# The order of VectorE's small column copies in items of one tile of a mixture-of-experts loop

## The chip, the cores and the metric

The kernel runs on one core of one Trainium2 chip. A time is the device time of one execution in microseconds (us), and a kernel's time is the median of several executions. The engines are TensorE (PE, with its weight loads PEld), VectorE (DVE), ScalarE (ACT), GpSimd (POOL) and SyncE (SP). Each takes its own instructions in order and waits on semaphores for the others.

## The reference

Attention over keys and values that are averaged in groups of 8 rows, and after it a mixture of experts in which each of the 4608 rows goes to one of 8 experts, the one with the largest gate. An expert takes at most `capacity` rows (4608 / 8 * 2 = 1152), in the order of the rows; a row beyond that stays zero.

```python
logits = x @ w_gate                       # x: 4608 x 512, from the attention
expert_idx = np.argmax(logits, axis=1)
gate_w = probs[np.arange(N), expert_idx]  # softmax of logits
...
h = np.maximum(np.einsum('ecd,edf->ecf', disp, w1), 0.0)   # 8 experts, 512 -> 1024
y = np.einsum('ecf,efd->ecd', h, w2)                       # 1024 -> 512
...
out[i] = gate_w[i] * y[expert_idx[i], pos[i]]              # zero where a row was not kept
```

## The kernel before

The first 212 us are the attention, the routing and a prologue that already computes two tiles of one expert. Behind it stands a loop (lines 1327 to 1372) over items. An item is one or two tiles of 128 rows of one expert; how many, which columns of the tables belong to it, and whether the expert changes behind it are read from the table `cf` as the loop runs, so the code of the loop has branches: `two` chooses between an item of two tiles (`hidden_all`) and of one (`hidden_one`), and `sw` says that the next item is another expert's, so that its weights are split in this one.

All matrix products are made in three terms: each operand is split into a rounded high part (names with h: `xh`, `w1h`, `hh`, `w2h`; a cast on ScalarE, line 127) and the remainder (`xl`, `w1l`, `hl`, `w2l`; a subtraction on VectorE, line 128 or 1299). TensorE multiplies high by high, high by low and low by high.

What one item does, by engine:

- TensorE: the hidden layer (line 152, or 1309 and the transposes of 1314 where there is one tile) into `ph`, for two tiles the product of tile 1 into `y1`, the transposes of the next item's rows (line 1286, `xg` into `px`), and the product of tile 0 into `y0` (line 165). The next item's hidden layer follows at once; it needs `xh` and `xl` of its rows, and after `sw` the new `w1h` and `w1l`. `w1l` is split in four instructions: two for the first 512 columns of the hidden layer and two for the rest.
- VectorE: the remainders `hl` of the hidden layer, then three small copies of int32 columns by dynamic offset: `ix`, the row numbers that the gather after next needs (128x4, line 92), `io`, the row numbers and gates of this item's own rows (128x4, line 92), and `iz`, the rows beyond capacity that get zeros (128x2, line 1360). Further the remainders `xl` of the next item's rows, after `sw` the `w1l` and `w2l`, and the gates (line 1321) that scale `y` into `ys`.
- POOL: at the item's start it overwrites `io` and `iz` with zeros (lines 1336 and 1337), which it may do once the scatters of the item before, which read `io` and `iz`, have landed. Then it makes a guard, a tiny subtraction that waits for VectorE's `ix` (line 95), issues two gathers of 128 rows into `xg` (line 97, after TensorE's transposes have read `xg`), a guard on `iz` and two scatters of zero rows, guards on `io` and on `ys`, and two scatters of result rows into `out` (line 102).
- SP: the weights of the expert after next into `r`, two loads for the first layer (line 120) and two for the second (line 124), each once VectorE's and ScalarE's splits have read `r`.

VectorE's `io` and `iz` are written after POOL's zeros, so they wait for POOL's lines 1336 and 1337. Within the loop the order of each engine's instructions is that of the code.

## Time and profile before

| | us |
|---|---|
| median of 3 runs | 639.56 |
| the three runs | 635.9, 639.56, 639.87 |
| the profiled execution | 638.75 |
| its span, from the first to the last instruction | 637.1 |
| TensorE busy in the span | 600.0 |
| VectorE busy in the span | 335.4 |
| POOL busy in the span | 315.6 |

The profile is that of one execution. The view of the waits gives for each pair of instructions what one waited for, the us in total, how many times, and the longest. A row of the timeline has the start in us from the span's start, the duration (of several instructions in a row together), the engine, the line, the operation with what it writes and reads, and how many; in brackets stands the idle time of the engine ahead of it and what ended it. A row of the busy time by stretch has the stretch, its length, and for PE, PEld, DVE, ACT and POOL the busy us and the number of instructions, then the clock granted to TensorE (1.00 is full), the share of the DMA engines and GB/s. A row of one line has the shortest, the median and the longest duration in ns, and the first and the last start.

### The profile page before, as it was taken

The page shows a single profiled execution, that of the slowest core. Times are in us where ns is not written, and L with a number is a line of the kernel's source. Part 1 is how long each engine was busy: PE and PEld are TensorE (multiplying, and loading weights), DVE is VectorE, ACT ScalarE, POOL GpSimd, SP SyncE. Part 2 cuts the span into 40 slices and gives each one's busy share as a digit, 9 for nine tenths or more (in the row PEclk, how much of TensorE's full clock was granted, in tenths as well). Part 3 has the DMA queues.
Part 4 walks back from the last instruction along what each step waited for, and adds up shares of the span by engine and source line. Part 5 has one row for each costly group of instructions (what it writes and reads, how often), then busy time and mean ns, then how long its engine had stood idle before and what let it go on. Part 6 is the DMA issues. An engine that isn't in the chain of part 4 may idle for free. (4 is left out here: it accounts for less than half of the span.)

```text
span 637.1 us, 13935 instructions
## 1 busy us (share of the span) xinstructions
PE 600.0 (94%) x3966; PEld 534.0 (84%) x3967; DVE 335.4 (53%) x742; ACT 223.1 (35%) x412; POOL 315.6 (50%) x533
## 2 busy tenths in 40 slices
PE   2799999999889899999999999999999999999994
PEld 1688889898787789988889989988899889988983
DVE  4776968888878421359447622227322584223212
ACT  2456364556532211157155412117111581101111
POOL 7399959557664331445444541444324255341344
PEclk9899999999999999999999999999999999999998
DMA  9999899485622810137728720214501261110112
GB/s 314 305 338 278 240 305 198 93 248 127 181 52 76 311 54 33 66 133 277 241 96 287 260 100 33 66 51 163 189 33 66 77 247 36 66 66 6 60 51 65
DMA packets 103744, 93.79 MB, mean 147 GB/s; under 512 B 82852, under 2 KB 82852, under 8 KB 103720
## 3 DMA queue, kind: packets, MB, share of 16 engines
q1 hardware_dynamic: 54552, 62.47, 30.4%
q0 software_dynamic: 11392, 21.57, 10.7%
q10 hardware_dynamic: 37776, 9.46, 6.8%
q8 instruction: 12, 0.20, 0.1%
q14 instruction: 12, 0.10, 0.0%
HBM read 132.96 MB, written 31.27 MB: 258 GB/s over the span
## 5 line engine op out<-in xcount | busy, mean ns | idle before, releaser
L1299 DVE SCALAR_TENSOR_TENSOR hl<-ph,hh 128x512 fp32r<-128x512 f32 x60 | 40.9, 691 | 108.0 <-ACT hh L1298 75.7
L1298 ACT ACTIVATE hh<-ph 128x512 fp32r<-128x512 f32 x60 | 36.0, 599 | 173.8 <-PE ph L152 168.2
L152 PE MATMUL ph<-xh,w1h 128*128 128x256 f32 x480 | 76.5, 281 | 2.8 <-DVEq L1327 2.5
L165 PE MATMUL y<-w2h,hh 128*128 128x512 f32 x280 | 78.1, 400 | 0.0
L165 PE MATMUL y<-w2l,hh 128*128 128x512 f32 x280 | 76.6, 395 | 0.0
L152 PE MATMUL ph<-xl,w1h 128*128 128x256 f32 x480 | 76.2, 281 | 0.4 <-DVE w1l L128 0.4
L152 PE MATMUL ph<-xh,w1l 128*128 128x256 f32 x480 | 76.1, 280 | 0.0
L97 POOL DMA_INDIRECT xg<-xs,ix x42 | 44.3, 1056 | 58.8 <-PE y L165 51.6
L165 PE MATMUL y<-w2h,hl 128*128 128x512 f32 x280 | 71.0, 396 | 0.0
L152 PEld LDWEIGHTS ph<-xh,w1h 128*128 128x128 f32 x480 | 65.8, 188 | 5.8 <-issue 4.8
L152 PEld LDWEIGHTS ph<-xl,w1h 128*128 128x128 f32 x480 | 65.1, 188 | 0.7 <-issue 0.7
L152 PEld LDWEIGHTS ph<-xh,w1l 128*128 128x128 f32 x480 | 65.1, 188 | 0.0
L165 PEld LDWEIGHTS y<-w2h,hl 128*128 128x128 f32 x280 | 52.6, 188 | 12.7
L165 PEld LDWEIGHTS y<-w2l,hh 128*128 128x128 f32 x280 | 52.6, 188 | 12.6
L549 PE MATMUL pa<-vbd,pT 126*128 126x146 f32 (+5 forms) x400 | 58.2, 306 | 1.1 <-DVE pairs L704 0.7
L165 PEld LDWEIGHTS y<-w2h,hh 128*128 128x128 f32 x280 | 50.0, 188 | 9.4
L549 PEld LDWEIGHTS pa<-vbd,pT 126*128 126x128 f32 (+1 forms) x400 | 54.7, 179 | 3.5 <-issue 1.7
L128 DVE TENSOR_TENSOR xl<-px,xh 128x512 fp32r<-128x512 f32 x40 | 25.7, 685 | 56.8 <-ACT xh L127 56.8
L95 POOL TENSOR_TENSOR guard<-ix 128x4 int32<-128x4 int32 x21 | 6.1, 292 | 99.9 <-DVE ix L92 87.6
L538 ACT COPY pT<-pp 126x384 f32<-126x384 f32 x72 | 30.5, 424 | 68.6 <-PE pp L537 53.4
L513 PE MATMUL ps<-kbs,qT 128*128 128x144 f32 (+1 forms) x320 | 52.0, 305 | 1.9 <-ACT qT L504 1.9
L102 POOL DMA_INDIRECT out_dram<-zrow,iz x40 | 45.9, 1147 | 15.8 <-issue 15.2
(263 smaller groups left out, 1021.6 us busy)
## 6 DMA issues: line engine op xcount, KB each, us to landing
r<-in_moe_w_dram SPq DMA_DIRECT2D x84, 1024.0 KB
raw<-in_k_dram SPq DMA_DIRECT2D x12, 768.0 KB
raw<-in_v_dram SPq DMA_DIRECT2D x12, 768.0 KB
qblk<-in_q_dram SPq DMA_DIRECT2D x32, 256.0 KB
xs<-xo ACTq DMA_DIRECT2D x16, 512.0 KB
raw<-in_moe_w_dram SPq DMA_DIRECT2D x4, 512.0 KB
r<-in_moe_w_dram SPq DMA_DIRECT2D x4, 512.0 KB
qtail<-in_q_dram SPq DMA_DIRECT2D x8, 128.0 KB
```

Of the source, the lines that this page charges most:

```text
L95: nc.gpsimd.tensor_sub(guard, ix, ix)
L97: nc.gpsimd.indirect_dma_start(out=dst[:, i, :].bitcast(F32), out_offset=None, in_=src, in_offset=bass.IndirectOffsetOnAxis(ap=ix[:, i, 0: ...
L102: ins = nc.gpsimd.indirect_dma_start(out=out[:, :], out_offset=bass.IndirectOffsetOnAxis(ap=i_, axis=0), in_=src, in_offset=None, bounds_c ...
L128: eng.tensor_sub(lo, src, hi.bitcast(F32))
L152: nc.tensor.matmul(p[:, f2], a[:, c, f * P : (f + 1) * P], b[:, c], start=(f2 == 0 and j == 0 and c == 0), stop=(f2 == 1 and j == 2 and c ...
L165: nc.tensor.matmul(y, a[:, c, i * P : (i + 1) * P], b[:, c], start=(first and n == 0), stop=(last and n == len(terms) - 1))
L513: nc.tensor.matmul(self.ps[us, h, 0 : 2 * SP_].rearrange("p (a x) -> p a x", a=2), self.qT[:, h, us], kbs[b // 2 % 2][:, :, b % 2, h], sta ...
L538: nc.scalar.copy(self.pT[:, cs.start : cs.stop], pp[0:KC, 0 : len(cs)])
L549: made = nc.tensor.matmul(self.pa[us, h0 * XW : (h0 + nh) * XW], self.pT[:, c, us], vbd[b % 2][:, c, 0:nh].rearrange("r s x -> r (s x)"), ...
L1298: nc.scalar.activation(hh[s], p, AF.Relu)
L1299: nc.vector.scalar_tensor_tensor(out=hl[s], in0=p, scalar=0.0, in1=hh[s].bitcast(F32), op0=ALU.max, op1=ALU.subtract)
```

## The change

In items of one tile VectorE's copy of `ix` moves from behind the remainders `hl` to the very start of the item. Its copies of `io` and `iz` move from behind the split of the first weights to right after `hl`, ahead of the remainders `xl` of the next rows. In items of two tiles only `iz` moves: from behind the gate of tile 1 to ahead of it. No instruction is added or taken away, apart from branches; no transfer changes.

```diff
-                def next_x():
+                def next_ids():
                     columns(ix, ids[:, ds(c2, 2), :])
-                    gather(xg, ix, xs[:, :])
-                    split_x()
+
+                def own_ids():
+                    columns(io, ids[:, ds(ct, 2), :])
+                    nc.vector.tensor_scalar(out=iz, in0=idd[:, ds(cd, 2)], scalar1=0, scalar2=None, op0=ALU.bitwise_or)
...
                     with tc.If(sw > 0):
                         split_w1()
-                    next_x()
-                    columns(io, ids[:, ds(ct, 2), :])
+                    next_ids()
+                    gather(xg, ix, xs[:, :])
+                    split_x()
+                    own_ids()
                     gate(1)
                 with both.Else():
+                    next_ids()
                     hidden_one()
-                    next_x()
+                    gather(xg, ix, xs[:, :])
+                    own_ids()
+                    split_x()
                     with tc.If(sw > 0):
                         split_w1()
-                    columns(io, ids[:, ds(ct, 2), :])
                 load_w1(we, cond=nw > 0, bounds_check="skip_entire_dma")
-                nc.vector.tensor_scalar(out=iz, in0=idd[:, ds(cd, 2)], scalar1=0, scalar2=None, op0=ALU.bitwise_or)
```

VectorE in the branch for one tile, from the remainders `hl` on, as it was. In the brackets are the engines and the DMA queues that a row waits for; REGISTER_ALU and ISA rows only prepare a wait or an offset:

```order
L128 TENSOR_TENSOR hl<-ph_2826,hh 128x4x128 [waits Activation_I-2847_own]
L128 REGISTER_ALU
L128 TENSOR_TENSOR hl<-ph_2827,hh 128x4x128 [waits Activation_I-2847_own]
L92 ISA
L92 TENSOR_SCALAR ix<-ids 128x4 [waits DMASW0_I-2847_own,DMASW1_I-2847_own,DVE_I-2847_own,Pool_I-2847_own]
L128 REGISTER_ALU
L128 TENSOR_TENSOR xl<-px_2822,xh 128x4x128 [waits Activation_I-2847_own]
L128 REGISTER_ALU
L128 TENSOR_TENSOR xl<-px_2823,xh 128x4x128 [waits Activation_I-2847_own]
L1356 COMPARE_AND_BRANCH
```

The same branch of VectorE now, from its start on:

```order
L92 TENSOR_SCALAR ix<-ids 128x4 [waits DMASW0_I-2847_own,DVE_I-2847_own,DMASW1_I-2847_own,Pool_I-2847_own]
L128 REGISTER_ALU
L128 TENSOR_TENSOR hl<-ph_2826,hh 128x4x128 [waits Activation_I-2847_own]
L128 REGISTER_ALU
L128 TENSOR_TENSOR hl<-ph_2827,hh 128x4x128 [waits Activation_I-2847_own]
L92 ISA
L92 TENSOR_SCALAR io<-ids 128x4 [waits DMASW4_I-2847_own,DMASW5_I-2847_own,DVE_I-2847_own,Pool_I-2847_own]
L1344 ISA
L1344 TENSOR_SCALAR iz<-idd 128x2 [waits DMASW3_I-2847_own,DMASW2_I-2847_own,Pool_I-2847_own]
L128 REGISTER_ALU
L128 TENSOR_TENSOR xl<-px_2822,xh 128x4x128 [waits Activation_I-2847_own]
```

`ix` stands ahead of `hl`, and `io` and `iz`, with their waits for the landing of scatters (DMASW4 and 5, DMASW3 and 2) and for POOL, stand ahead of `xl` and so ahead of the `w1l` that follow `xl`.

TensorE at the start of the hidden layer of an item of two tiles, as it was:

```order
L152 MATMUL ph_2824<-xh,w1l 128x256 [waits DVE_I-2847_own]
L152 MATMUL ph_2824<-xh,w1l 128x256
L152 REGISTER_ALU
L152 MATMUL ph_2824<-xh,w1l 128x256 [waits DVE_I-2847_own]
L152 MATMUL ph_2824<-xh,w1l 128x256
L152 REGISTER_ALU
L152 MATMUL ph_2824<-xl,w1h 128x256 [waits DVE_I-2847_own,DVE_49]
L152 MATMUL ph_2824<-xl,w1h 128x256 x3
```

And the same place now:

```order
L152 MATMUL ph_2824<-xh,w1l 128x256 [waits DVE_I-2847_own]
L152 MATMUL ph_2824<-xh,w1l 128x256
L152 REGISTER_ALU
L152 MATMUL ph_2824<-xh,w1l 128x256 [waits DVE_I-2847_own]
L152 MATMUL ph_2824<-xh,w1l 128x256
L152 MATMUL ph_2824<-xl,w1h 128x256 [waits DVE_49]
L152 MATMUL ph_2824<-xl,w1h 128x256 x3
L152 MATMUL ph_2824<-xh,w1h 128x256 x4
```

TensorE's matmuls stand as before; the first of the `xl` group no longer waits for a count of VectorE within the loop, since the waits of the `w1l` group ahead of it, one for each half of the rows of the first weights, cover it.

## The prediction

> **What bounds the kernel now.** I read four views: the page's first lines, the waits of each engine from 212 us on (the loop over the items), the busy time by stretch, and then the timeline around each item of one tile. Times with three digits before the point are us from the start of the span.

> ```profile
> span 637.1 us, 13935 instructions
> PE 600.0 (94%) x3966; PEld 534.0 (84%) x3967; DVE 335.4 (53%) x742; ACT 223.1 (35%) x412; POOL 315.6 (50%) x533
> ...
> PE ph L152 <- DVEq L1327: 2.5, 1, 2.5
> PE ph L152 <- DVE w1l L128: 0.4, 2, 0.2
> ...
> POOL guard L95 <- DVE ix L92: 87.6, 16, 12.2
> POOL io L1336 <- DMA out_dram<-ys,io: 59.2, 19, 6.3
> ...
> 299.00:326.00 27.00, 27.00 (x161) 23.65 (x161) 10.86 (x16) 5.22 (x10) 15.56 (x25) 1.00 0.66 226
> ...
> L128 DVE TENSOR_TENSOR hl<-ph,hh x10: 681/692/692, 291.5 to 622.9; 128x512 fp32r<-128x512 f32 x10
> ```

> In the loop TensorE is the bound: its only waits on another engine are 2.5 us as the loop begins and two waits on `w1l`, 0.4 us together; the stretch from 299 to 326 us is full of matmuls. So what delays TensorE moves the end by as much, and what frees another engine is worth nothing until the last item, where TensorE runs out of work. POOL idles 87.6 us for VectorE's index columns and 59.2 us for the landing of the scatters, off that path. The ten `hl` splits of line 128 are two for each item of one tile: five such items. In order of time I call them A (292 us), B (328), C (434), D (517) and E (623). In A to D the next expert's first weights are split too; E is the last item and splits none.

> **Part 1: `io` and `iz` stand ahead of the remainders `xl`.** VectorE takes its instructions in order. The new `io` must wait until POOL has zeroed `io` (L1336), and that waits for the landing of the item before's result rows. Behind it now stand two `xl` and four `w1l`. Item A before, by engine and start:

> ```profile
> 286.82 1.80 POOL L102 DMA_INDIRECT out_dram<-ys,io  x1 [0.15 <-issue]
> 291.45 1.29 DVE L128 TENSOR_TENSOR hl<-ph,hh 128x512 fp32r<-128x512 f32 x2 [1.43 <-ACT hh L127]
> 292.73 1.28 DVE L128 TENSOR_TENSOR xl<-px,xh 128x512 fp32r<-128x512 f32 x2
> 293.93 4.62 DVE L128 TENSOR_TENSOR w1l<-r,w1h 128x1024 fp32r<-128x1024 f32 x4
> 294.24 0.96 POOL L1336 TENSOR_TENSOR io<-zi 128x4 int32<-128x4 int32 x1 [5.62 <-DMA out_dram<-ys,io]
> 295.15 1.18 POOL L1337 TENSOR_TENSOR iz<-zi 128x2 int32<-128x2 int32 x1
> 296.73 0.63 PE L152 MATMUL ph<-xh,w1l 128*128 128x256 f32 x4
> 297.56 0.72 PE L152 MATMUL ph<-xl,w1h 128*128 128x256 f32 x4 [0.20 <-DVE w1l L128]
> ```

> VectorE reaches this place at 291.45 + 1.29 = 292.74. POOL's zeroing starts at 294.24 only, 5.62 us after the scatter's issue ended (286.82 + 1.80 = 288.62). Nothing ahead of that landing is changed, so I keep 294.24. POOL's two zeroings took 0.96 and 1.18 here, beside a `w1l`; with VectorE waiting I take the 0.19 that they need in item E (below), the second 0.15 after the first: done at 294.58. A hand-over from VectorE to POOL costs 0.14 there; I take the same the other way, and 0.07 from the last column to the next instruction: the first `xl` starts at about 294.24 + 0.55 = 294.79. From `xl`, the first `w1l` follows after 1.20 (293.93 - 292.73), the next after 1.135 (4.62 less one of 1.22, by 3), so the second `w1l`, which completes the first half of the weights, ends 3.55 after `xl`. TensorE reads that half in the third and fourth matmul of its `w1l` group, and the `xl` group starts 0.24 later. With 0.14 for the hand-over, the `xl` group starts at the landing + 0.55 + 3.55 + 0.14 + 0.24 = landing + 4.48 = 298.72, where before it started at 297.56. Its old wait of 0.20 is inside that, since the order of TensorE shows that group's own wait gone. **A: +1.16.** That the index columns come first takes away 0.07 of VectorE's time there, inside the same sum.

> Item D is the same case:

> ```profile
> 512.30 1.80 POOL L102 DMA_INDIRECT out_dram<-ys,io  x1 [0.15 <-issue]
> 516.93 1.29 DVE L128 TENSOR_TENSOR hl<-ph,hh 128x512 fp32r<-128x512 f32 x2 [1.42 <-ACT hh L127]
> 518.20 1.28 DVE L128 TENSOR_TENSOR xl<-px,xh 128x512 fp32r<-128x512 f32 x2
> 520.09 0.58 POOL L1336 TENSOR_TENSOR io<-zi 128x4 int32<-128x4 int32 x1 [5.99 <-DMA out_dram<-ys,io]
> 522.24 0.63 PE L152 MATMUL ph<-xh,w1l 128*128 128x256 f32 x4
> 523.03 0.71 PE L152 MATMUL ph<-xl,w1h 128*128 128x256 f32 x4 [0.16 <-DVE w1l L128]
> ```

> VectorE is there at 516.93 + 1.29 = 518.22, the rows land for 520.09, TensorE's group starts at 520.09 + 4.48 = 524.57 and not at 523.03. **D: +1.54.**

> In B and C POOL has zeroed long before VectorE comes:

> ```profile
> 325.45 0.19 POOL L1336 TENSOR_TENSOR io<-zi 128x4 int32<-128x4 int32 x1 [1.88 <-DMA out_dram<-ys,io]
> 328.69 0.16 DVE L92 TENSOR_SCALAR ix<-ids 128x4 int32 x1
> 328.76 1.28 DVE L128 TENSOR_TENSOR xl<-px,xh 128x512 fp32r<-128x512 f32 x2
> 329.91 0.98 POOL L97 DMA_INDIRECT xg<-xs,ix  x1 [0.71 <-PE y L165]
> 330.06 4.66 DVE L128 TENSOR_TENSOR w1l<-r,w1h 128x1024 fp32r<-128x1024 f32 x4
> 333.62 0.64 PE L152 MATMUL ph<-xh,w1l 128*128 128x256 f32 x4
> ```

> In B the zeroings end by 325.45 + 0.34 = 325.79 and VectorE comes at 328.69, a cover of 2.9 us; C goes like B. Two column instructions cost 0.07 to 0.25 ahead of `xl`; the second `w1l` ended at 330.06 + 1.22 + 1.14 = 332.42 and TensorE came to it at 333.62 + 0.24, so 1.4 us of cover is left: **0**. If that cover were gone, the cost would be at most those 0.25.

> What stands behind `w1l` on VectorE comes later by as much as `xl`, 294.79 - 292.73 = 2.06 us: the gate of the result, the `w2l` splits, and with the splits SP's two weight loads, which wait until they free their buffers. In A:

> ```profile
> 299.44 4.62 DVE L128 TENSOR_TENSOR w2l<-r,w2h 128x1024 fp32r<-128x1024 f32 x4
> 309.13 1.09 PE L165 MATMUL y<-w2l,hh 128*128 128x512 f32 x4
> ```

> The last `w2l` would end at 299.44 + 4.62 + 2.06 = 306.12, and TensorE reads the first at 309.13, itself 1.16 later: a cover of 4 us. The loads are wanted at the next split of first weights, at 330.06: **0**. In items of two tiles `iz` goes ahead of the gate of tile 1, one instruction of 0.16 ahead of a result that only POOL's scatter reads: **0**.

> **Part 2: the next index columns come first.** POOL can issue the two gathers as soon as it has zeroed and TensorE has transposed the rows. For TensorE this is early by tens of us in A to D: 0. It counts in E, where POOL's chain ends the program:

> ```profile
> 619.53 1.00 POOL L102 DMA_INDIRECT out_dram<-ys,io  x1 [2.04 <-issue]
> 622.40 0.19 POOL L1336 TENSOR_TENSOR io<-zi 128x4 int32<-128x4 int32 x1 [1.88 <-DMA out_dram<-ys,io]
> 622.55 0.19 POOL L1337 TENSOR_TENSOR iz<-zi 128x2 int32<-128x2 int32 x1
> 623.54 0.16 DVE L92 TENSOR_SCALAR ix<-ids 128x4 int32 x1
> 623.84 0.20 POOL L95 TENSOR_TENSOR guard<-ix 128x4 int32<-128x4 int32 x1 [1.10 <-DVE ix L92]
> 624.76 0.98 POOL L97 DMA_INDIRECT xg<-xs,ix  x1 [0.72 <-PE y L165]
> 627.94 0.75 DVE L1321 TENSOR_SCALAR ys<-y,io 128x512 f32<-128x512 f32 x1 [2.18 <-PE y L165]
> 631.30 0.21 POOL L1371 TENSOR_TENSOR guardf<-ys 128x2 f32<-128x2 f32 x1
> 631.67 1.00 POOL L102 DMA_INDIRECT out_dram<-ys,io  x1 [0.16 <-issue]
> ```

> POOL is free at 622.55 + 0.19 = 622.74 and waits 1.10 for the columns made at 623.54 (end 623.70, then 0.14 to POOL's start: the hand-over above). With columns made ahead of the item's own remainders, the guard starts at 622.75, and all behind it moves by 1.09: POOL is busy or in short issue gaps from there to 631.67. The last scatter needs VectorE's gate, done at 627.94 + 0.75 = 628.69; it would start at 630.58, so the cover is 1.9 us. **E: -1.09.** What could lessen it is the first gather's own wait, 0.72, which the row puts down to TensorE. Bounds 0 and -1.09; I take the full one, since B's gather stands 0.71 behind its guard too, which looks like a fixed gap and not like a wait that ends by chance.

> **The sum** is 1.16 + 1.54 - 1.09 = +1.61 us on the profiled execution of 638.75 (span 637.1 and 1.65 around it): 640.4. That execution lies 0.81 below the median of the three runs, 639.56; they spread from 635.9 to 639.87. About 1% (6.4 us) is what a measurement of this kernel can tell from no change.

> [...] The landing of 5.6 and 6.0 us is the weightiest row: E has 1.88. [...] The second row is B's gather at 329.91, started 0.15 ahead of a `w1l`. [...]

> **The rivals.**
> 1. The scatters land early in A and D, as in E. Then neither item waits, 0.20 and 0.16 of old waits go, and E gains: 638.75 - 0.36 - 1.09 = 637.3. It decides when the landing in A is before 293.1. Against it: the scatters and the weight loads beside them are issued by the item before, where nothing of this changes. 0.12.
> 2. POOL's gap of 2.04 us ahead of its scatter at 619.53, put down to nothing but issue (0.16 ahead of the last one), is not met again, and E starts 1.88 earlier on POOL. The last scatter can then come no earlier than the gate lets it: 628.69 + 0.14 + 0.37 from its guard's start = 629.20, a gain of 2.47 in place of 1.09: 639.0. 0.10.
> 3. The first gather of E is held by TensorE, not by VectorE: E gains nothing: 641.45. 0.08.
> 4. Gathers and `w1l` take turns in A and D. The gathers now come at about 295.5 (294.58 + 0.20 + 0.71) and a gather later, on top of the first two `w1l`: up to 0.98 more in each item, 640.4 + 1.96 = 642.4. Against it: B's `w1l` that started 0.15 into a gather. 0.05.
> 5. Slower by over 1%, by one mechanism: VectorE's wait for the landing is much longer than before's trace has it. Over 1% needs +1.16 + 1.54 to become 7.5, 2.4 us more in each: landings 8.0 and 8.4 us after the issue. The longest wait of POOL for a landing is 6.3 (the row above); with that in both items the time is only 0.68 + 0.31 more, 641.4. 0.04.

> **How the numbers follow.** The forecast, a stall in A and D less the gain in E, has 0.60; the five rivals 0.39; 0.01 is left for what I have not seen. The range runs from rival 1 to rival 4, each let out by the 0.81 between the profiled run and the median: 636.5 to 643.2. All but rival 5 lie within 1% of the median, so: same 0.92, slower 0.05 (rival 5 and a trace of unseen costs), faster 0.03 (rivals 1 and 2 together give 635.9, which is within 1%, so this is for the unseen alone).

> **What would show it.** In the changed profile: VectorE's `io` in A and D idle until POOL's zeroing, and `xl` behind it; TensorE waiting over 1 us for `w1l` twice; POOL's zeroing back at 0.19 there; in B and C no wait; in E the guard right behind the zeroing and the last scatter some 1.1 us nearer to the last matmul. Wrong would be a landing in A or D that comes before VectorE, a wait of TensorE anywhere else, or a guard in E that still waits.

## The result, and the profile after

| | before | changed |
|---|---|---|
| median, us | 636.37 | 640.07 |
| executions | 22 | 22 |
| the profiled execution, us | 638.75 | 643.0 |
| its span, us | 637.1 | 641.0 |

The ratio of changed to before is 1.006, with a 95% interval of 1.0038 to 1.0081: the change costs 2.4 to 5.2 us, less than 1%. One execution of before took 674.5 us, 5% more than any other, and is left out of the ratio. That the forecast of 640.4 is near the median of 640.07 is luck: it starts from one execution of 638.75, 2.4 us above the median of before, and adds +1.61 us where +3.8 us (0.006 x 636.4) was measured. The two errors, 2.4 us too much and 2.2 us too little, cancel.

The first lines of the profile after, with the span and the busy time of the engines:

```profile
span 641.0 us, 13947 instructions
PE 605.9 (95%) x3966; PEld 540.2 (84%) x3967; DVE 334.2 (52%) x742; ACT 222.9 (35%) x412; POOL 317.0 (49%) x533
```

TensorE does the same 3966 instructions and is busy 5.9 us longer, its weight loads 6.2; POOL is busy 1.4 us longer, VectorE and ScalarE are not. So TensorE is not only waiting more, some of its instructions are also slower. The waits in the loop, from 205 us on (engine and line, whom it waited for, us in total, times, longest):

```profile
POOL guard L95 <- DVE ix L92: 98.8, 14, 12.8
POOL io L1336 <- DMA out_dram<-ys,io: 61.3, 19, 6.8
POOL guard L1366 <- DVE w1l L128: 11.0, 4, 3.9
DVE io L92 <- POOL io L1336: 4.1, 2, 2.1
PE ph L152 <- DVE w1l L128: 3.6, 4, 1.3
PE ph L152 <- DVEq L1327: 2.5, 1, 2.5
```

VectorE now waits twice for POOL's zeroing, 4.1 us, and TensorE four times for `w1l`, 3.6 us where it was 0.4: two waits in A and two in D. The third row was not foreseen: POOL's guard on `iz` waits for `w1l` in four items of one tile, 11.0 us, so having `iz` early there does nothing for POOL. It costs nothing either, as POOL is not on the path there.

Item A after, rows of the timeline by engine:

```profile
286.66 2.65 SPq L124 DMA_DIRECT2D r<-in_moe_w_dram  x2
...
286.67 1.80 POOL L102 DMA_INDIRECT out_dram<-ys,io  x1 [0.15 <-issue]
295.17 0.19 POOL L1336 TENSOR_TENSOR io<-zi 128x4 int32<-128x4 int32 x1 [6.71 <-DMA out_dram<-ys,io]
...
291.91 0.17 DVE L92 TENSOR_SCALAR ix<-ids 128x4 int32 x1 [3.18 <-issue]
295.39 0.17 DVE L92 TENSOR_SCALAR io<-ids 128x4 int32 x1 [2.07 <-POOL io L1336]
295.72 1.29 DVE L128 TENSOR_TENSOR xl<-px,xh 128x512 fp32r<-128x512 f32 x2
...
296.15 0.72 PE L152 MATMUL ph<-xh,w1h 128*128 128x256 f32 x4
298.20 0.51 PE L152 MATMUL ph<-xh,w1l 128*128 128x256 f32 x2 [1.33 <-DVE w1l L128]
299.33 0.50 PE L152 MATMUL ph<-xh,w1l 128*128 128x256 f32 x2 [0.62 <-DVE w1l L128]
299.67 0.63 PE L152 MATMUL ph<-xl,w1h 128*128 128x256 f32 x4
300.61 1.02 PE L152 MATMUL ph<-xh,w1l 128*128 128x256 f32 x4
302.28 1.05 PE L152 MATMUL ph<-xh,w1h 128*128 128x256 f32 x4
```

The chain is the one forecast: the rows land, POOL zeroes in 0.19, `io` follows 0.22 later, `xl` and `w1l` behind it, and TensorE's `xl` group starts at 299.67, which is 4.50 behind the zeroing's start (forecast 4.48). Two things are not: the landing takes 6.71 in place of the 5.62 that I kept, and 0.9 us behind the start of that group TensorE's groups of four matmuls take 1.05 in place of 0.63. That is its clock:

```profile
297.00:323.00 26.00, 24.18 (x146) 21.88 (x147) 14.69 (x20) 6.15 (x9) 13.52 (x18) 0.93 0.60 206
```

This is the busy time by stretch; the third number from the end, the granted clock, is 0.93 in the 26 us behind A, where it was 1.00 before. In D the landing took 6.36, the `xl` group started 4.50 behind the zeroing, and the clock stayed at 1.00 (from 524 to 550 us):

```profile
523.67 0.19 POOL L1336 TENSOR_TENSOR io<-zi 128x4 int32<-128x4 int32 x1 [6.36 <-DMA out_dram<-ys,io]
...
528.17 0.63 PE L152 MATMUL ph<-xl,w1h 128*128 128x256 f32 x4
```

The last rows of item E:

```profile
627.25 0.19 POOL L1336 TENSOR_TENSOR io<-zi 128x4 int32<-128x4 int32 x1 [1.88 <-DMA out_dram<-ys,io]
627.80 0.20 POOL L95 TENSOR_TENSOR guard<-ix 128x4 int32<-128x4 int32 x1 [0.21 <-issue]
635.62 1.00 POOL L102 DMA_INDIRECT out_dram<-ys,io  x1 [0.16 <-issue]
...
632.87 0.75 DVE L1321 TENSOR_SCALAR ys<-y,io 128x512 f32<-128x512 f32 x1 [2.98 <-PE y L165]
```

The guard no longer waits for VectorE, and the last scatter starts 635.62 - 632.87 = 2.75 us behind the gate, where it was 631.67 - 627.94 = 3.73: a gain of 0.98 of the 1.09 forecast. What is missing is an issue gap of POOL, 0.21, which appears in front of the guard where the forecast had 0.01; in turn the gate stands 0.08 later behind POOL's zeroing than before (5.62 against 5.54), which leaves 0.11.

Followed along the path, the profiled executions differ by +2.11 in A (299.67 against 297.56, with TensorE reaching the item at the same time), +1.84 in D, -0.98 in E, +1.20 between A and D, and -0.2 elsewhere: +3.95 us on the last scatter's start (635.62 against 631.67).

For all executions together I use two numbers: the **clock loss**, span times (1 - mean granted clock), and the **rest**, span less clock loss. Both come from the span and clock that each run lists. A stretch of 3.41 us at half clock, which the record of the clock gives as 0.50, is a loss of 1.7 us. In both profiles a part of the clock loss costs no time: TensorE runs out of work 9.2 us before the end in that of before (at 627.83 of 637.1) and 8.2 in the changed one, and half clock is granted there too (before from 632.66 on, 2.2 of the 3.9 us lost in that profile). So about half of E's gain of 1 us stands in the clock loss, and not in the rest.

### The profile page after: what moved, and what is told of

It is laid out like the page before. It is cut to its first block, busy times and chain, and to the rows that moved or that the text cites. A ratio compares the mean times of both kernels' runs of the same rounds, so it can differ in the third digit from the quotient of the medians.

```text
span 641.0 us, 13947 instructions
## 1 busy us (share of the span) xinstructions
PE 605.9 (95%) x3966; PEld 540.2 (84%) x3967; DVE 334.2 (52%) x742; ACT 222.9 (35%) x412; POOL 317.0 (49%) x533
## 5 line engine op out<-in xcount | busy, mean ns | idle before, releaser
L152 PE MATMUL ph<-xh,w1l 128*128 128x256 f32 x480 | 77.9, 284 | 3.6 <-DVE w1l L128 3.6
L152 PE MATMUL ph<-xh,w1h 128*128 128x256 f32 x480 | 77.4, 284 | 2.8 <-DVEq L1327 2.5
L165 PE MATMUL y<-w2h,hh 128*128 128x512 f32 x280 | 78.0, 400 | 0.0
L152 PE MATMUL ph<-xl,w1h 128*128 128x256 f32 x480 | 76.8, 282 | 0.0
L165 PE MATMUL y<-w2l,hh 128*128 128x512 f32 x280 | 76.6, 395 | 0.0
L97 POOL DMA_INDIRECT xg<-xs,ix x42 | 41.3, 983 | 63.0 <-PE y L165 54.0
L152 PEld LDWEIGHTS ph<-xh,w1h 128*128 128x128 f32 x480 | 66.7, 191 | 5.7 <-issue 4.8
L165 PE MATMUL y<-w2h,hl 128*128 128x512 f32 x280 | 71.0, 395 | 0.0
L152 PEld LDWEIGHTS ph<-xh,w1l 128*128 128x128 f32 x480 | 66.2, 191 | 4.4 <-DVE w1l L128 4.4
L152 PEld LDWEIGHTS ph<-xl,w1h 128*128 128x128 f32 x480 | 65.9, 191 | 0.0
L165 PEld LDWEIGHTS y<-w2h,hl 128*128 128x128 f32 x280 | 52.6, 188 | 12.7
L165 PEld LDWEIGHTS y<-w2l,hh 128*128 128x128 f32 x280 | 52.6, 188 | 12.6
L165 PEld LDWEIGHTS y<-w2h,hh 128*128 128x128 f32 x280 | 50.0, 188 | 9.4
L128 DVE TENSOR_TENSOR xl<-px,xh 128x512 fp32r<-128x512 f32 x40 | 25.8, 686 | 57.7 <-ACT xh L127 57.7
L513 PE MATMUL ps<-kbs,qT 128*128 128x144 f32 (+1 forms) x320 | 53.3, 310 | 1.9 <-ACT qT L504 1.9
L95 POOL TENSOR_TENSOR guard<-ix 128x4 int32<-128x4 int32 x21 | 4.1, 197 | 99.7 <-DVE ix L92 98.8
L102 POOL DMA_INDIRECT out_dram<-zrow,iz x40 | 47.8, 1196 | 9.3 <-issue 9.3
```

Of the source, the lines that this page charges most:

```text
L95: nc.gpsimd.tensor_sub(guard, ix, ix)
L97: nc.gpsimd.indirect_dma_start(out=dst[:, i, :].bitcast(F32), out_offset=None, in_=src, in_offset=bass.IndirectOffsetOnAxis(ap=ix[:, i, 0: ...
L102: ins = nc.gpsimd.indirect_dma_start(out=out[:, :], out_offset=bass.IndirectOffsetOnAxis(ap=i_, axis=0), in_=src, in_offset=None, bounds_c ...
L128: eng.tensor_sub(lo, src, hi.bitcast(F32))
L152: nc.tensor.matmul(p[:, f2], a[:, c, f * P : (f + 1) * P], b[:, c], start=(f2 == 0 and j == 0 and c == 0), stop=(f2 == 1 and j == 2 and c ...
L165: nc.tensor.matmul(y, a[:, c, i * P : (i + 1) * P], b[:, c], start=(first and n == 0), stop=(last and n == len(terms) - 1))
```

## The experiments

Times are medians; the ratio is to the kernel before on the same chip. "Rest" and "clock" are the differences of the mean rest and the mean clock loss from that kernel's; they are uncertain by 0.2 to 0.5 and by 0.4 to 1.3 us (one standard error).

| run | us | ratio, 95% interval | rest | clock | TensorE waits for `w1l` in the profile, us (times) |
|---|---|---|---|---|---|
| e1, ix first alone | 636.43 | 1.0003 (0.9982 to 1.0024) | +0.07 | +0.03 | 1.2 (2) |
| e2, io and iz early alone | 640.4 | 1.0082 (1.0048 to 1.0116) | +2.31 | +2.58 | 3.7 (4) |
| e3, io and iz behind xl | 636.84 | 1.0007 (0.9984 to 1.0029) | +0.54 | -0.23 | 1.6 (3) |
| e4, no weight loads in the loop | 634.42 | one run | | | 0 |
| e5, TensorE kept busy | 644.09 | 1.0085 (1.0052 to 1.0118) | +6.43 | -1.46 | 0 |
| e6, old order, a short delay | 644.98 | 1.0108 (1.0059 to 1.0157) | +5.72 | +1.29 | 4.2 (6) |
| e7, ix first, gate in quarters | 639.63 | 1.0002 (0.9979 to 1.0026) | -1.08 | +0.75 | 0.2 (1) |
| e8, iz where it was | 640.01 | 1.0017 (0.9991 to 1.0043) | +0.51 | +0.18 | 0.8 (2) |
| e9, old order, a longer delay | 664.16 | 1.0448 (1.0414 to 1.0482) | +15.94 | +12.30 | 7.5 (12) |
| e10, ix between the hl | 634.54 | 0.9995 (0.9972 to 1.0018) | -0.25 | -0.17 | 0.2 (1) |
| e11, before again | 635.21 | 0.9992 (0.9968 to 1.0016) | -0.09 | -0.33 | 0.9 (2) |
| e12, changed again | 639.52 | 1.0065 (1.0037 to 1.0092) | +1.67 | +2.16 | 3.2 (4) |

e1 to e4 ran on one chip, e5 to e8 on a second, e9 and e10 on a third, e11 and e12 on a fourth.

### The parts alone: e1, e2, e3

e1 keeps `ix` first and puts the item's own columns back:

```diff
                     gather(xg, ix, xs[:, :])
-                    own_ids()
                     split_x()
                     with tc.If(sw > 0):
                         split_w1()
+                    own_ids()
```

> The changed kernel, but in items of one tile io and iz go back behind the split of the first weights; ix stays first. Theory (the loss is VectorE's wait for the landing of the scatters ahead of xl in items A and D, plus a lower TensorE clock behind it): no wait of TensorE for w1l above 0.3 us, the last scatter starts 2.7 to 2.8 us after the last gate starts (3.73 before, 2.75 with the change), time about 1 us below the kernel before, ratio to it 0.997 to 1.000. Rival (having ix first is what costs, since VectorE now stands at the start of the item): the ratio stays near the change's 1.006.

e2 keeps the own columns early and puts `ix` back behind `hl`:

```diff
-                    next_ids()
                     hidden_one()
+                    next_ids()
```

> The changed kernel, but in items of one tile ix goes back behind hl; io and iz stay ahead of xl. Theory: the same waits as with the change, in A and D together 2.5 to 4 us of TensorE, xl group of TensorE at the landing + 4.48 (within 0.15), and the gain at the end of 1 us is lost: ratio to before 1.005 to 1.010. Rival (ix first costs): ratio 1.000 to 1.003. Rival on the clock (the dips of the granted clock come anywhere and have nothing to do with the waits): no dip just behind A or D.

e3 keeps everything but has `xl` ahead of the own columns, so that only `w1l` stands behind them:

```diff
-                    own_ids()
                     split_x()
+                    own_ids()
```

> The changed kernel, but io and iz stand between xl and the split of the first weights, so that only w1l is behind the wait. Theory: the xl group of TensorE starts at the landing + 3.28, 1.2 us sooner than with the change: waits of TensorE for w1l in A and D together 0.4 to 2 us, ratio 0.998 to 1.004, between the first experiment and the change. Rival (any place of io ahead of the w1l costs the same, because the count of VectorE's instructions that TensorE waits for is what matters): waits and ratio as with the change.

The whole loss belongs to part 1: e2 loses as much as the whole change, within the intervals, and e1 nothing that can be measured. In e2 the waits are those of the changed kernel:

```profile
DVE io L92 <- POOL io L1336: 4.2, 2, 2.2
PE ph L152 <- DVE w1l L128: 3.7, 4, 1.5
```

e2 has part 1 without the gain in E (gate to last scatter 3.72 us); its rest is +2.31, against +1.67 for the whole change (e12, on another chip). In e1 that distance is 2.91, a gain of 0.8 that the time does not show. Its own waits for `w1l`, 0.59 in A and 0.58 in D, are above the 0.3 that I had set, against 0.20 and 0.16 in the first profile of before: `ix` at the item's start comes late (below). But the unedited kernel had 0.72 and 0.15 in e11, so I cannot say that `ix` first caused them.

In e3 VectorE does 1.29 us of `xl` while it would wait. What is left of the waits is shorter for that, the rest is +0.54 in place of +1.67, and the clock loss is not above before's. The `xl` group stood 3.56 and 3.57 us behind the landing, not 3.28: `w1l` started 0.19 us behind the end of `iz`, put down to ScalarE's `w1h` in A and to issue in D. The waits of e3:

```profile
PE ph L152 <- DVE w1l L128: 1.6, 3, 0.6
DVE io L92 <- POOL io L1336: 0.9, 2, 0.6
```

### Why the landing is late: e4

The changed kernel without the loads of weights in the loop:

```diff
-                load_w1(we, cond=nw > 0, bounds_check="skip_entire_dma")
...
-                load_w2(we, cond=nw > 0, bounds_check="skip_entire_dma")
```

> The changed kernel without the weight loads in the loop (both layers), so that every expert after the second is computed with stale weights. Theory (the landing of the result rows is late in A and D because they stand behind the weight loads on the DMA engines): POOL's wait for the landing falls from 6.4 to 6.7 us to about 1.9 us in A and D, VectorE's io waits for nothing, TensorE waits for w1l 0.3 us or less. Rival (the landing is late because POOL's scatter itself is slow there, 1.80 us beside w2l): the landing stays above 5 us and the waits stay.

In A and in D POOL's zeroing then starts 1.88 and 1.89 us behind the scatter's issue:

```profile
288.01 0.19 POOL L1336 TENSOR_TENSOR io<-zi 128x4 int32<-128x4 int32 x1 [1.88 <-DMA out_dram<-ys,io]
512.93 0.19 POOL L1336 TENSOR_TENSOR io<-zi 128x4 int32<-128x4 int32 x1 [1.89 <-DMA out_dram<-ys,io]
```

TensorE does not wait for `w1l` at all there. The scatter's own issue in A still took 1.80 us beside `w2l`, so that is not the reason. It is the loop's weight loads that hold the rows, for 5.3 to 7.2 us in A and D of the other thirteen profiles, and without them rival 1 would have come about.

### Is it the wait that brings the clock down? e5, e6, e9

e5 is the changed kernel with 16 unused matmuls behind `hidden_one` (0.118 us each), so that TensorE works while it would wait:

```diff
                     hidden_one()
+                    for _ in range(16):
+                        nc.tensor.matmul(ph[0][:, 0:256], identr, wr["h"][:, 0, 0:256], start=True, stop=True)
```

> The changed kernel with 16 matmuls of 128x256 added behind the hidden layer of every item of one tile; their result is not used. By the changed kernel's rows one takes 0.118 us, so 1.89 us an item. In A and D they fill the time in which TensorE waited for the second half of the first weights (1.95 and 1.60 us there), in B and C, which had no wait, they add 1.89 each, in E at most 0.9. Theory (a third to a half of the loss is TensorE's clock, which falls to half for 3.4 us after a wait of some 2 us): waits for w1l in A and D under 0.6 together, no stretch of half clock behind A, clock loss (span times one less the mean granted clock) back from 6.3 us to about 4.3, span less clock loss up by 4 to 5 us from 632.1, median about 642.5. Rival (the clock is lower for a reason other than the waits): clock loss still over 5.5 us, median about 644.5.

The waits are gone, and there is no extra clock loss: 2.9 us (6 runs) against 4.35 for before on that chip. The median of 644.09 is nearer to the rival's figure, but the kernel before takes 638.42 on that chip, some 3 us more than on the others. The clock behind A is full:

```profile
293.00:323.00 30.00, 30.00 (x183) 26.48 (x182) 16.75 (x25) 10.33 (x14) 16.32 (x24) 1.00 0.69 231
```

By itself this does not show that the matmuls took a clock loss away. The changed kernel was not run on that chip, where the landings were earlier (5.63 and 5.71), and e8 below, which is the change but for one move, had waits of only 0.8 us there and no extra clock loss either.

e6 and e9 are the old order with 4 and with 10 unread multiplications ahead of `ix` in items of one tile, so VectorE is late without any landing:

```diff
                     hidden_one()
+                    for _ in range(4):
+                        nc.vector.tensor_scalar_mul(idle, idle, 1.0)
                     next_x()
```

> The kernel before with four VectorE multiplications of a 128x512 tile of its own, which nobody reads, ahead of the next index columns in items of one tile. A gate of that size takes 0.75 us in the trace, so some 2.4 to 3.0 us. This delays xl and w1l without any landing. Theory (what costs is that VectorE comes late to xl, and a long wait of TensorE brings the clock down): TensorE waits 2 to 3 us in A and D each, 0.8 to 1.6 in B and C, a stretch of half clock of about 3.4 us behind A and D, mean clock loss over 6 us against 4.3, and the end 2.4 to 3.0 us later on POOL's chain in E: median +9 to +13 us. Rival (the landing or the order of the columns itself matters to the clock): waits of the same length, but clock loss stays below 5 us; median +7 to +9.

> The kernel before with ten instead of four of the unread multiplications (0.43 us each in the run with four) ahead of the next index columns in items of one tile. By that run's rows VectorE reaches xl 2.6 us later than there: TensorE waits 3.9 us in A and D (0.63 + 0.72 there) and 2.6 to 3.3 in B and C (0.72 there), and E's last scatter is 2.6 us later; span less clock loss +18 to +19 us over before. Theory (the clock is set by stretches of 3.41 us on a fixed grid, and one in which TensorE idles for more than about 1.9 us is followed by one at half clock; up to 1.5 it is not): at least two and up to four stretches of half clock behind A to D, each behind a stretch with over 1.6 us idle, clock loss 8 to 12 us, median +21 to +27. Rival (a half clock in the loop needs something of the changed order, and not the wait): no half clock behind A to D, clock loss 4 to 6, median +18 to +20.

e6 missed: one multiplication took 0.43 us, not 0.6 to 0.75, the waits were 1.35 us in A and in D (two pieces) and 0.72 in B and C, no half clock followed in its profile, and with 4 runs its clock loss (+1.29, uncertain by 1.3) says nothing; the median was 6.6 us over before, under the range of either theory. So it told no theory from the other, and e9 was made longer. In e9 TensorE waits 2.8 to 3.9 us in each of A to D, in pieces; in A these four and one of 1.2 ahead of them:

```profile
294.42 0.72 PE L152 MATMUL ph<-xh,w1h 128*128 128x256 f32 x4 [0.80 <-DVE xl L128]
295.74 0.50 PE L152 MATMUL ph<-xh,w1l 128*128 128x256 f32 x2 [0.60 <-DVE w1l L128]
296.88 0.50 PE L152 MATMUL ph<-xh,w1l 128*128 128x256 f32 x2 [0.64 <-DVE w1l L128]
298.10 1.19 PE L152 MATMUL ph<-xl,w1h 128*128 128x256 f32 x4 [0.72 <-DVE w1l L128]
```

The busy time around B and around D, with the granted clock at 0.83 and at 1.00:

```profile
332.00:352.00 20.00, 17.20 (x102) 15.13 (x101) 16.01 (x24) 8.01 (x10) 9.85 (x11) 0.83 0.64 222
528.00:548.00 20.00, 16.26 (x103) 13.41 (x102) 17.16 (x27) 11.57 (x15) 8.23 (x9) 1.00 0.49 155
```

Half clock followed in A (3.41 us), B (6.83) and C (6.83), and not in D. The rival, that the changed order itself is needed, falls. The mean loss of 16.2 us is more than the 8 to 12 forecast, and the median 28.9 us over before is more than the 21 to 27; two of the stretches were double, which is 3.4 us of loss in this profile.

### Does the move of iz make the landing later? e8, e10, e11, e12

In the first two profiles the gate of tile 0 in the item ahead of A started at 284.73 before and at 283.44 after. SP's second weight loads stand 3.22 behind that gate, so they started 1.13 us behind the last scatter's issue before (287.95 against 286.82) and beside it after (286.66 against 286.67), and the landing took 5.62 and 6.71. I took the move of `iz` in items of two tiles for the cause. e8 undoes that move alone:

```diff
-                    nc.vector.tensor_scalar(out=iz, in0=idd[:, ds(cd, 2)], scalar1=0, scalar2=None, op0=ALU.bitwise_or)
...
                 load_w1(we, cond=nw > 0, bounds_check="skip_entire_dma")
+                nc.vector.tensor_scalar(out=iz, in0=idd[:, ds(cd, 2)], scalar1=0, scalar2=None, op0=ALU.bitwise_or)
```

> The changed kernel with iz alone back where it was, behind the join of the two branches; ix first and io ahead of xl stay. Theory (the move of iz lets the gate of tile 0 in the items ahead of A and D go 1.3 us earlier, with it the w2l splits and the second weight loads, and these loads then delay the landing of the result rows): the gate of tile 0 waits 4.2 us again there in place of 3.1, the loads start about 1.2 us behind the last scatter's issue and not beside it, landing 5.6 to 6.0 us after that issue in A in place of 6.7, TensorE's wait in A 0.8 to 1.0 us shorter, under 1.2 us. Rival 1 (the gate goes early for another reason, such as ix or io): the gate waits 3.1, landing 6.4 to 6.9, TensorE's wait in A 1.9 to 2.1. Rival 2 (the gate is late again but the landing does not follow it): gate 4.2, landing 6.4 to 6.9.

```profile
288.17 0.38 SPq L124 DMA_DIRECT2D r<-in_moe_w_dram  x1
...
287.04 1.80 POOL L102 DMA_INDIRECT out_dram<-ys,io  x1 [0.15 <-issue]
294.77 0.19 POOL L1336 TENSOR_TENSOR io<-zi 128x4 int32<-128x4 int32 x1 [5.94 <-DMA out_dram<-ys,io]
```

The loads came 1.13 behind the scatter, the landing took 5.94, and TensorE waited 0.52 in A and 0.29 in D: it looked like a confirmation, and its time was only 0.17% above before (the changed kernel itself was not run on that chip). But e5, e6 and e7, on the same chip and with other orders, `iz` moved in e5 and e7, had loads 1.1 us behind and landings of 5.3 to 5.8 as well, and e10 below, with `iz` unmoved but on another chip, had the loads beside the scatter in both items. So I ran both unedited kernels on one chip.

> The kernel before, unedited, profiled on the same chip as the changed kernel. In the runs so far the gate of tile 0 ahead of A and D came at the end of TensorE's y (a wait of about 3.0 us) in all profiles of two chips, among them one of the old order with iz unmoved, and up to 1.3 us later (3.1 to 4.2 us, put down to TensorE's next group or to issue) in all profiles of a third chip, whatever the order. Theory (the chip decides when the gate goes, and with it whether the second weight loads start beside the last scatter or 1.1 us behind it): this kernel and the changed one show the same gate wait, within 0.3 us, and landings of the same kind, both 5.5 to 6.0 with late loads or both 6.1 to 6.9 with early ones. Rival (the move of iz decides): this kernel late (4.2 us, loads 1.1 us behind the scatter, landing in A 5.6), the changed one early (3.1 us, loads beside it, 6.4 to 6.9).

> The changed kernel, unedited, on the same chip as the kernel before. Theory (the chip decides): gate wait as in the kernel before here. If it is late, landing 5.6 to 5.9 in A, TensorE's xl group 4.48 us behind that landing and 1.0 to 1.5 us later than before in A and in D, as forecast; if it is early, 6.4 to 6.9 and 1.8 to 2.3 us. Half clock behind A only where a stretch of the 3.41 us grid has over 1.6 us of idle TensorE. Rival (iz decides): gate wait 3.1, landing 6.4 to 6.9, on any chip. Ratio 1.002 to 1.007 in both cases.

The kernel before there, ahead of A and in A:

```profile
280.67 0.75 DVE L1321 TENSOR_SCALAR ys<-y,io 128x512 f32<-128x512 f32 x1 [2.73 <-PE y L165]
...
285.02 1.80 POOL L102 DMA_INDIRECT out_dram<-ys,io  x1 [0.15 <-issue]
293.48 0.70 POOL L1336 TENSOR_TENSOR io<-zi 128x4 int32<-128x4 int32 x1 [6.66 <-DMA out_dram<-ys,io]
...
293.38 0.72 PE L152 MATMUL ph<-xh,w1h 128*128 128x256 f32 x4
295.41 0.71 PE L152 MATMUL ph<-xl,w1h 128*128 128x256 f32 x4 [0.72 <-DVE w1l L128]
```

And the changed kernel on that chip:

```profile
278.58 0.75 DVE L1321 TENSOR_SCALAR ys<-y,io 128x512 f32<-128x512 f32 x1 [3.06 <-PE y L165]
...
281.80 1.80 POOL L102 DMA_INDIRECT out_dram<-ys,io  x1 [0.15 <-issue]
290.54 0.19 POOL L1336 TENSOR_TENSOR io<-zi 128x4 int32<-128x4 int32 x1 [6.94 <-DMA out_dram<-ys,io]
...
291.29 0.72 PE L152 MATMUL ph<-xh,w1h 128*128 128x256 f32 x4
293.57 0.50 PE L152 MATMUL ph<-xh,w1l 128*128 128x256 f32 x2 [1.56 <-DVE w1l L128]
294.70 0.50 PE L152 MATMUL ph<-xh,w1l 128*128 128x256 f32 x2 [0.63 <-DVE w1l L128]
295.05 0.63 PE L152 MATMUL ph<-xl,w1h 128*128 128x256 f32 x4
```

The gate goes at the end of `y` in both, and the landing in A is late in both, 6.66 and 6.94; in D it was 6.72 and 5.80, where 6.4 or more was expected of an early gate. The theory of `iz` falls: the order of the copies does not decide the landing. Gate and loads went the same way in all profiles of one chip, and landings were 5.3 to 6.0 where the loads came 1.1 us behind (10 items) and 5.6 to 7.2 where they came beside or ahead (16 items, two of them under 6.0). In some of these 26 the view puts POOL's wait down to a VectorE instruction that ended at about the same time; the trace has the scatter's last count 0.17 or 0.18 us ahead of the zeroing in each. What in a chip or an execution sets the gate's time stays open.

On one chip the `xl` group now starts 3.76 behind the first group of the item in A (295.05 - 291.29) against 2.03, so +1.73; in D +1.28 in the same way. E gains 0.96. That makes +2.05 in these two profiles; over all runs the rest is +1.67, uncertain by 0.4.

### Looking for a version that beats both: e7, e10

e7 is e1 with the gate of tile 1 in four pieces, so that the count on which TensorE's `xl` group waits is met by the second `w1l`:

```diff
-                    gate(1)
+                    for c in range(0, DM, P):
+                        s = slice(c, c + P)
+                        nc.vector.tensor_scalar_mul(ys[1][:, s], y[1][:, s], io[:, 1, 1:2].bitcast(F32))
```

> The kernel in which the next index columns come first and the item's own columns stay behind the split of the first weights, with the gate of tile 1 in four pieces of 128x128, so that VectorE's two branches have counts at which TensorE's wait of the xl group is met by the second w1l. Theory: TensorE's waits for w1l in A and D fall from 0.59 and 0.58 to at most 0.3, no half clock in the loop, last scatter 2.8 to 2.9 us behind the start of the last gate (3.73 before): ratio 0.996 to 0.999. Rival (the delay of hl by the index columns at the item's start costs as much as the gain at the end): waits stay at 0.5 or more, ratio 0.999 to 1.002.

e10 is the kernel before with one edit, `ix` between the two `hl` of `hidden_one`:

```diff
                 split(hh[s], hl[s], p)
                 if f == 0:
                     transpose_x()
+                    columns(ix, ids[:, ds(c2, 2), :])
```

> The kernel before with one edit in items of one tile: the next index columns stand between the two remainders hl. io and iz stay where they were, in both kinds of item. Theory (only the index columns of E are worth anything, and at the very start of the item they delay hl): no wait of TensorE for w1l over 0.3 us, the gate of tile 0 ahead of A and D waits 4.2 us as before, landing 5.6 to 6.0, the last scatter starts 2.9 to 3.2 us behind the start of the last gate in place of 3.73, no half clock behind A or D; ratio 0.997 to 1.000, a gain of 0.5 to 0.8 us, too small to be told from none. Rival (the order of the columns in E is worth nothing because the gathers are held by TensorE): last scatter 3.6 to 3.8 behind.

Both do what they should in the profile: one wait of 0.15 us in e7 and one of 0.25 in e10, and gate to last scatter 2.98 and 2.91. In e10, item E:

```profile
618.12 0.20 POOL L95 TENSOR_TENSOR guard<-ix 128x4 int32<-128x4 int32 x1 [0.21 <-DVE ix L92]
626.01 0.99 POOL L102 DMA_INDIRECT out_dram<-ys,io  x1 [0.16 <-issue]
```

Neither can be told from the kernel before: a gain of 0.8 us lies inside intervals of 0.2% to either side. The early gate of e10 contradicted its expectation, as said above.

## Why the prediction came out as it did

- **The stall in A and D** is right, and so is its formula. The `xl` group starts 4.48 us behind the landing by the forecast; it was 4.50 in A and D of the changed profile and 4.51 in A and in D of e12. POOL's zeroing is back at 0.19, as forecast.
- **"Nothing ahead of that landing is changed, so I keep 294.24"** holds as to the code: e11 has the late landing without the change. What was wrong was to keep the 5.62 and 5.99 of one execution as if they were the kernel's. Landings in these two items went from 5.3 to 7.2 over the profiles with loads. In the first pair the later ones make A dearer by 0.95 (2.11 less 1.16) and D by 0.30 (1.84 less 1.54).
- **B and C** have no wait of TensorE for `w1l`, and the `w2l` and loads behind cost nothing, as forecast. The move of `iz` in items of two tiles, costed at 0, is not what sets gate and landing: e11 and e12, on one chip, have an early gate and a late landing in A alike.
- **E: -1.09** measured -0.98 and -0.96; the lack comes from POOL's issue gap of 0.21 ahead of the guard. Rival 3 falls, since the guard went early and everything moved with it. Rival 2 falls: the gap ahead of the scatter at the end of the item before E was met again, 2.60 us in the changed profile.
- **Rival 1** needs the loads away (e4). **Rival 4** falls: the four `w1l` of A take 4.62 with the gathers beside them (0.99 and 1.06 long), as before. **Rival 5** was near in its mechanism, but the longest landing of the changed kernel was 6.94 (7.18 in e9), short of the 8.0 that it needed.
- **The sum, "1.16 + 1.54 - 1.09 = +1.61 us"**, is the step that failed, by a term that is not in it. The prediction says that "what delays TensorE moves the end by as much"; with the clock it moved the end by nearly twice as much. What the sum counts, time at full clock, came out near: +2.05 in the profiles of e11 and e12, and a rest of +1.67, uncertain by 0.4, over their runs. The other half is TensorE's clock: +2.16 us there, uncertain by 0.9, and 6.3 us of mean clock loss in the 22 runs of the changed kernel, where the kernel before has 3.9 to 4.4 on the four chips. (The half of E's gain that stands in the clock loss would shift some 0.5 us from the rest to the clock.) I counted a wait of TensorE at its length, and the clock that falls behind it at nothing. That the wait brings it rests on e9, where half clock follows long waits in the old order, on e2, which has the waits and the extra loss (+2.58), on e3, whose shorter waits, 0.99 us in A and 0.63 in D, bring none, and on the table of all profiles below; e5 agrees. With the clock's 2.2 us the sum is +3.8, and +3.8 was measured, with an interval of 2.4 to 5.2. The total of 640.4 was right by luck, as its start was 2.4 us too high.

## What to carry to other kernels

A copy of a few columns that waited for a transfer held back everything behind it on its engine (VectorE waited 4.1 us at `io`, and TensorE 3.6 for `w1l` where it was 0.4): put such a copy behind the work that the critical engine waits for, and count its wait from the landing beside the loads that run then, over more than one profile (5.3 to 7.2 us in A and D here, 1.88 without the loads). Waits of TensorE can cost nearly twice their length, since the clock may fall for 3.4 us behind one of some 2 us (e2: +2.31 us of rest and +2.58 of clock loss); the waits of e3, up to 0.99 us in an item, cost only themselves (+0.54 and -0.23). POOL, off the path, gained only where the program ends on it, 0.98 us in E.

## What the runs showed of the hardware

| idle in a stretch of 3.413 us | stretches | followed by half clock |
|---|---|---|
| 1.9 us and more | 11 | 11 |
| 1.59 to 1.81 us | 10 | 4 |
| 1.3 to 1.51 us | 9 | 0 |

Four of the eleven in the first row are at the end, where TensorE runs out of work. The table fits the changed profile: of the wait in A (1.95 us) 1.59 fell in one stretch, of that in D (1.60) 1.41, and half clock followed in A alone. So it matters where a wait falls on the grid. In the second row the four that were followed all hold waits for `w1l` in A (changed, e2, e9, e12), and the six that were not stand at the loop's start or at the end; what decides there was not tried. Half clock followed each stretch that was idle for 1.9 us or more of its 3.413, 11 of 11.

**VectorE's first copy of an item came late.** `ix` at the start of A came 3.18 us (3.34 in e12) behind the last `w2l`, put down to issue, and 0.11 ahead of an `hl` that before had started at 291.45, so 0.57 earlier at the same position of TensorE. The prediction had `hl` unmoved; the wait for the landing hid the delay. VectorE reads five values of the table `cf` there first (lines 1329 to 1335). That these reads are the 3 us was not tested.

**Some of POOL's work took longer beside the split of weights.** POOL's last scatter ahead of A takes 1.80 us beside `w2l` and 1.00 in E. Its small subtractions ended 0.05 us behind splits that ran beside them: in A of the first profile the four `w1l` start at 293.93, last 1.22 and follow each other by 1.135, so the first two end at 295.15 and 296.28, and POOL's zeroings beside them, 0.96 and 1.18 long in place of 0.19, end at 295.20 and 296.33. Against rival 4 the prediction holds a `w1l` of B that started 0.15 us into a gather's issue. That shows only that this `w1l` did not wait for that gather.
